# ACT reads a finished product sum one instruction earlier, ahead of the last score tile's exponential, in thirteen stretches of a fused attention and token-mixer kernel

## The chip, the cores and the metric

One Trainium2 chip, one core of it. The metric is the device time of the kernel in microseconds (us), the median of several runs, so lower is better. Names of the engines: PE is the matrix engine, PEld its weight-load port, DVE the vector engine, ACT the scalar (activation) engine, POOL the GpSimd engine, SP the engine that issues the DMAs.

## The reference

Two branches read the same tokens `x` (2048 tokens, 640 channels) and a gate per token mixes them. Branch A is attention with 32 query heads of width 20 that share one key and one value head. Branch B is a token mixer: a layer norm, then an MLP across the token axis.

```python
# A: q is (32 heads, 2048, 20), k and v are (2048, 20), all from x
scores = jnp.einsum("bhqd,bkd->bhqk", q, k) * (Dh ** -0.5)
p = _softmax(scores, axis=-1)
a = (jnp.einsum("bhqk,bkd->bhqd", p, v)) ... @ wo
# B: h is layernorm(x); u is (640, 1728), y is (640, 2048)
u = _gelu(jnp.einsum("bsd,sf->bdf", h, w1) + b1)
y = jnp.einsum("bdf,fs->bds", u, w2) + b2
g = _sigmoid((x * gate_w).sum(-1, keepdims=True))
out = g * a + (1 - g) * y.transpose
```

Everything is float32. The kernel splits the operands of most products into a high and a low part, so each product becomes three matmuls that add into one PSUM tile.

## The kernel before, in words

The order of every engine's instructions is written out by hand (a manual schedule over all five engines): an engine executes them in the order in which the Python code emits them, and waits where an operand or a buffer isn't ready.

After a first part that makes q, k, v and the layer norm, the kernel runs a list `ph` of 326 **stretches**. `main(k, vs)` emits stretch k. It has two lanes on PE, one for each half of the rows of the array, and `merged` interleaves them by modelled times:

- One lane holds twelve 512-column matmuls: six that recompute scores for the row maxima (`ms_next`, line 479, each followed by a DVE reduction, line 482) and six that compute score tiles (`s_next`, which calls `qk`, line 657, each followed by the exponential on ACT, line 660, which reads the score tile from PSUM and writes a tile `p`).
- The other lane holds about sixteen matmuls of branch B (the "fill"), here line 750: pieces of y = W2 u for one block of 128 tokens. They add into the PSUM tile `g`.

A stretch ends with the products p times v of one or two finished score units (`pv_mm`, line 684): one unit when k is even, two when k is odd.

Three points matter for the change.

1. The product sum `g` has one PSUM bank only (`ps_g`, one buffer). For the first thirteen token blocks (`st < FIVE`) each of the two channel halves (d = 0 and d = 1) takes five stretches (`five(d)`). At the end of the fifth, `done(d)` (line 758) makes ACT read `g` with scale and bias into the tile `yo`. The next stretch starts a new sum in the same bank, so its first fill matmul waits for that read. For d = 0 the fifth stretch has an even k, for d = 1 an odd one.
2. The score tiles and the tiles of the row maxima go round six PSUM banks in turn (`next_bank`: three named `ms`, three named `s`). A matmul into a bank waits until the reader of the tile six calls before has finished.
3. `done` stands in the order after the fill, and the last score step of the stretch stands ahead of the last fill matmul. So ACT gets: exponential, exponential of the last score tile, then the read of `g`.

Of the kernel before, what the change touches and what calls it, by code (L numbers as in the profile page):

```python
# [11 lines left out]
AF = mybir.ActivationFunctionType  # L12
# [23 lines left out]
SCALE = DH ** -0.5  # L36
# [3 lines left out]
def mix_kernel(ctx: ExitStack, tc: tile.TileContext, A_x, A_wq, A_wk, A_wv, A_wo,  # L40
               B_x, B_w1, B_b1, B_w2, B_b2, gate_w, out):
    nc = tc.nc
# [3 lines left out]
    def f32(ap):  # L46
        return ap.bitcast(F32)
# [107 lines left out]
    def new_q(n):  # L155
        if n < NU:
            qtiles[n] = load_q(n, "qst")
# [13 lines left out]
    with tc.tile_pool(name="pa", bufs=1) as pa, \  # L171
# [129 lines left out]
        def q_parts(m, ts):  # L301
            cols = slice(m * P, (m + 1) * P)
            return [[(wq_hi[:, c, cols], ts[c][0]) for c in range(DC)],
                    [(wq_hi[:, c, cols], ts[c][1]) for c in range(DC)],
                    [(wq_lo[:, c, cols], ts[c][0]) for c in (0, 3, 1, 4, 2)]]
# [88 lines left out]
        for sb in range(NQB):  # L394
# [11 lines left out]
            for m in range(DC):  # L406
# [3 lines left out]
                p = q_parts(m, ts)  # L410
# [48 lines left out]
    def next_bank():  # L459
        if not ring:  # L460
            return ps_m.tile([P, NB], F32, name="ms")
        ring[0] ^= 1
        return ps_m.tile([P, NB], F32, name="ms") if ring[0] else ps_s.tile([P, NB], F32, name="s")
# [25 lines left out]
    def ms_done():  # L489
        n = len(row_max)  # L490
        if n < NU and min(issued) >= 32 * (n + 1):
            mm = mmpool.tile([P, 16], F32, name="mm")
            nc.vector.tensor_reduce(mm, mtiles.pop(n), axis=AX.X, op=ALU.max)
            mn = mmpool.tile([P, 2, 16], F32R, name="mn")
            nc.gpsimd.tensor_scalar(mm, mm, -1.0, None, op0=ALU.mult)
            nc.gpsimd.tensor_copy(mn[:, 0, :], mm)
            nc.gpsimd.tensor_sub(mn[:, 1, :], mm, f32(mn[:, 0, :]))
            row_max[n] = mn
# [66 lines left out]
    with tc.tile_pool(name="psb", bufs=2, space=PSUM, side="right") as psb:  # L565
# [8 lines left out]
        for fc in range(PRO):  # L574
            pu = [psb.tile([P, NB], F32, name=f"pu{r}") for r in range(2)]
            for hf in range(4):
# [4 lines left out]
                for c in range(HS):  # L581
# [6 lines left out]
                    done = [max(0, min(x, last) - skip) * LEAD // (last - skip) for x in (at, at + 1)]  # L588
# [45 lines left out]
    SYNC = mybir.DependencyInfo(mybir.DependencyClass.Sync, mybir.DependencyReason.DATA)  # L634
    sc = [0, 0]
    turn_p = [0]

    def next_p():
        turn_p[0] += spare[0]
        i = turn_p[0] % 14  # L640
        return extra_p[i - 1] if 0 < i < 4 else pp_pool.tile([P, NB], F32, name="p")

    def s_next(b):
        j = sc[b]
        if j >= 2 * len(units):
            return None
        sc[b] += 1
        return lambda: qk(j // 2, j % 2, b)

    def qk(u, pr, b):  # L650
        n, kb = units[u]
        assert n in back_in
        if kb == 4 and pr == 0 and b == 0:
            new_q(n + 1)
        q = qtiles[n]
        s = ps_s.tile([P, NB], F32, name="s") if spare[0] else next_bank()
        nc.tensor.matmul(s, kst[64 * b:64 * b + 62, kb * P:(kb + 1) * P], q[64 * b:64 * b + 62, pr, :],  # L657
                         start=True, stop=True)
        p = next_p()
        nc.scalar.activation(p, s, AF.Exp, scale=SCALE)  # L660
        ptiles[u, 2 * pr + b] = p

    def other_tile(half, ins):
        if half is not None and last["half"] not in (half, None):
            tc.add_manual_dep(ins.ins, last["sig"].ins.name, SYNC, reason="row tiles that share a bank")
        last["half"], last["ins"] = half, ins
# [11 lines left out]
    def pv_mm(u):  # L678
        n, kb = units[u]
        if kb == 0:  # L680
            otile[0] = ps_o.tile([P, NB], F32, name="o")
        o = otile[0]
        for hh in range(4):
            nc.tensor.matmul(o[32 * hh:32 * hh + 32, :], v_sb[:, kb, :], ptiles.pop((u, hh)),  # L684
                             start=(kb == 0), stop=(kb == NS - 1), skip_group_check=True)
        if kb == NS - 1:
            qb, g = divmod(n, NQ)
            ot = ev.tile([P, NB // 32, 32], F32, name="ot")
            rl = ev.tile([P, NB // 32], F32, name="rl")
            on = ev.tile([P, NB], F32, name="on")  # L690
            oh = ev.tile([P, NB], F32R, name="oh")
            ol = ev.tile([P, NB], F32R, name="ol")
            direct = spare[0]
            src = o
            if not direct:
                src = on
                nc.scalar.activation(src, o, AF.Copy)

            def turn():
                nc.vector.transpose(ot.rearrange("p c e -> p (c e)"), src)  # L700

            def scale():
                if not direct:
                    turn()
                nc.vector.reciprocal(rl, ot[:, :, DH])  # L705
                (nc.vector if spare[0] else nc.gpsimd).tensor_mul(ot, ot, rl[:, :, None].to_broadcast([P, NB // 32, 32]))  # L706

            if direct:
                turn()

            def back():
                nc.vector.transpose(on, ot.rearrange("p c e -> p (c e)"))

            def high():
                osplit[:] = [oh, ol]
                if n < NU - 1:
                    nc.gpsimd.tensor_copy(oh, on)
                else:
                    nc.scalar.activation(oh, on, AF.Copy)

            def low():
                (nc.vector if n == NU - 1 else nc.gpsimd).tensor_sub(ol, on, f32(oh))
                for j, t in enumerate((oh, ol) if n < NU - 1 else ()):
                    for hh in range(4):
                        r = (4 * g + hh) * DH
                        nc.sync.dma_start(out=o_scr[j, r:r + DH, qb * NB:(qb + 1) * NB],
                                          in_=f32(t[32 * hh:32 * hh + DH, :]))

            if direct:
                later.append((False, None))  # L730
            later.extend(((True, scale), (True, back), (False, high), (False, low)))
# [222 lines left out]
    for i, (steps, rest, done) in enumerate(seq):  # L954
        item, j = divmod(i + 1, 3)
        rest.insert(0, lambda c=4 * (PRO + item) + (48 * j // 3) // 12: w1_upto(c + 4))
    def stretches(seq):
        return [(rows[1 - b], rest if b else [], done if b else []) for rows, rest, done in seq for b in range(2)]

    ph = stretches(seq)  # L960
# [29 lines left out]
    def merged(lx, lf):  # L990
        lanes, at, out = (list(lx), list(lf)), [0.0, 0.0], []
        while lanes[0] or lanes[1]:
            k = 0 if lanes[0] and (not lanes[1] or at[0] <= at[1]) else 1
            us, f = lanes[k].pop(0)
            if f:
                out.append(f)
            at[k] += us
        return out
# [18 lines left out]
    def main(k, vs):  # L1017
        b = k % 2
        fs, rest, done = ph[k]
        fill = [(F_US, f) for f in fs] + [(0.0, f) for f in [signal] + done]  # L1020
        if not vs:
            lx = [(3 * X_US, ms_next(b)), (3 * X_US, ms_next(b)), (X_US, s_next(b)), (X_US, ms_next(b))]
            lx += [(X_US, s_next(b)) for _ in range(3)]
            lf = fill + [(X_US, s_next(1 - b))]
        else:
            sx, sf = (MANY if len(fs) > 15 else FEW)[len(vs) == 1]
            lx = [(X_US, (s_next if c == "s" else ms_next)(b)) for c in sx]
            lf = []
            for c in sf:
                lf += fill if c == "F" else [(X_US, (s_next if c == "s" else ms_next)(1 - b))]  # L1030
        order = merged(lx, lf)
        known, kept = set(row_max), set(sent)
        wide = len(vs) == 2
        parted = wide and units[vs[0]][1] == NS - 1
        for i, f in enumerate(order):
            if wide and i == (len(order) + 1) // 2:
                settle()
                if parted:
                    pv_mm(vs[0])
            f()  # L1040
        ms_done()
        spare[0] = len(row_max) == NU
        settle(wide and not parted)
        if vs:
            n, kb = units[vs[0]][0] + 1, units[vs[0]][1]
            if n in kept and n not in back_in:
                fetch_max(n)
                back_in.add(n)
        for f in rest:
            f()  # L1050
        if vs and kb > 4 and n in known and n not in sent and n < NU:
            store_max(n)
            sent.add(n)
        for v in vs[parted:]:
            pv_mm(v)
# [16 lines left out]
    for n in BLOCKS:  # L1072
# [3 lines left out]
        i = 0  # L1076
        while any(sc[b] < ends[b] for b in range(2)):
            b = int(sc[1] < sc[0])
# [3 lines left out]
        fs = [tail_take(b, len(tail[b]) if n == left else  # L1082
                        max(0, round(((own[b] + len(tail[b]) * F_US) * n / left - len(lanes[b]) * X_US) / F_US)))
              for b in range(2)]
        at = [0.0, 0.0]
        while any(lanes) or any(fs):
            b = 0 if at[0] <= at[1] and (lanes[0] or fs[0]) or not (lanes[1] or fs[1]) else 1
# [76 lines left out]
```

## Time and profile before

| | |
|---|---|
| Time, median of 3 runs | 1671.76 us (1671.31 to 1671.92) |
| The profiled execution's own time | 1671.47 us |
| Its span, first to last instruction | 1669.7 us |
| Granted TensorE clock | 1.000 |
| Busy: PE / PEld / DVE / ACT / POOL | 99% / 66% / 86% / 71% / 36% |
| The stretches of the d = 0 and d = 1 sums above | about 689 to 1262 us of the span |

A row of the timeline reads: start in us, length in us, engine, line, operation, output<-inputs, shapes, count; in brackets stands how long the engine was idle before it, and what ended that. Matmuls are pipelined and overlap, so the sum of their lengths says little; their starts tell the rhythm.

### The profile page before, as it was taken

The numbers are of one execution on the slowest core, as the hardware profiler recorded it, in microseconds if no ns is written. First come the engines' busy times: TensorE is split into PE (matmuls) and PEld (weight loads), VectorE is DVE, ScalarE is ACT, GpSimd is POOL, SyncE is SP. The second block draws the span as 40 slices with busy tenths as digits, with TensorE's granted clock in tenths as the row PEclk, the third lists the DMA queues.
The fourth block names the chain that finished last, engine by engine and source line by source line (L and its number), as shares of the span: only waits on it lengthen the run. The fifth ranks groups of instructions, "written<-read, shape, count | busy, mean of one in ns | idle before, by whom it ended". The sixth has DMA issues, their size and how long they took to land.

```text
span 1669.7 us, 38827 instructions
## 1 busy us (share of the span) xinstructions
PE 1661.0 (99%) x14865; PEld 1105.5 (66%) x14865; DVE 1435.7 (86%) x2732; ACT 1188.0 (71%) x2346; POOL 606.3 (36%) x759
## 2 busy tenths in 40 slices
PE   9999999999999999999999999999999999999998
PEld 7899666666666666666666666666666566666665
DVE  6689899999989999988888988988888998988933
ACT  4434777777777777777777777777777777777775
POOL 6578555455455554422232332122122220111210
PEclk9999999999999999999999999999999999999999
DMA  7665222222132232222222222212222121333611
GB/s 211 205 176 137 79 71 69 78 58 78 53 84 73 71 82 74 58 60 62 66 75 74 55 62 66 61 52 71 63 66 60 55 65 41 96 111 113 189 51 39
DMA packets 178305, 138.20 MB, mean 83 GB/s; under 512 B 33306, under 2 KB 144055, under 8 KB 178119
## 3 DMA queue, kind: packets, MB, share of 16 engines
q1 hardware_dynamic: 177830, 135.39, 28.9%
q8 instruction: 117, 1.92, 0.5%
q14 instruction: 70, 0.57, 0.1%
q10 hardware_dynamic: 288, 0.33, 0.1%
HBM read 102.36 MB, written 31.65 MB: 80 GB/s over the span
## 4 chain that ended last, share of the span: by engine, by line
PE 95%; issue 2%; DVE 1%; SPq 1%; ACT 0%; DMA 0%; POOL 0%; POOLq 0%; DVEq 0%; ACTq 0%
PE o L684 28%; PE ms L479 18%; PE s L657 13%; PE g L750 10%; PE g L929 7%; PE ms L657 5%; PE pp L298 4%; PE s L479 3%; PE pu L586 3%; PE g L875 2%; DVE mp L482 1%; PE ms L831 0%; ACT p L660 0%; PE pt L290 0%; SPq L195 0%
## 5 line engine op out<-in xcount | busy, mean ns | idle before, releaser
L482 DVE TENSOR_REDUCE mp<-ms 128x1 f32<-128x512 f32 x1514 | 967.2, 685 | 130.2 <-PE ms L479 102.7
L660 ACT ACTIVATE p<-s 128x512 f32<-128x512 f32 x1512 | 820.6, 606 | 299.4 <-PE s L657 280.2
L479 PE MATMUL ms<-kst,qmx 60*128 60x512 f32 x1514 | 646.5, 433 | 1.7 <-DVE mp L482 1.7
L657 PE MATMUL s<-qst,kst 62*128 62x512 f32 x1512 | 601.6, 403 | 0.0
L684 PE MATMUL o<-p,v_sb 128*32 128x512 f32 x4096 | 511.3, 601 | 0.0
L479 PEld LDWEIGHTS ms<-kst,qmx 60*128 60x128 f32 x1514 | 279.0, 184 | 244.9 <-ACT p L660 114.7
L482 DVE TENSOR_REDUCE mp<-s 128x1 f32<-128x512 f32 x534 | 355.6, 683 | 12.0 <-PE s L479 11.8
L660 ACT ACTIVATE p<-ms 128x512 f32<-128x512 f32 x536 | 305.1, 599 | 56.8 <-PE ms L657 50.2
L657 PEld LDWEIGHTS s<-qst,kst 62*128 62x128 f32 x1512 | 278.5, 186 | 55.2 <-DVE flag L670 31.0
L929 PE MATMUL g<-slot,wh 64*128 64x320 f32 x1280 | 297.5, 311 | 0.0
L129 POOL TENSOR_TENSOR wl<-wr,wh 128x512 fp32r<-128x512 f32 x176 | 228.6, 1300 | 43.8 <-PE g L750 17.3
L479 PE MATMUL s<-kst,qmx 60*128 60x512 f32 x534 | 230.8, 441 | 0.4 <-DVE yo L525 0.4
L684 PEld LDWEIGHTS o<-p,v_sb 128*32 128x32 f32 x4096 | 97.5, 108 | 185.3 <-issue 177.2
L657 PE MATMUL ms<-qst,kst 62*128 62x512 f32 x536 | 216.8, 405 | 0.0
L929 PEld LDWEIGHTS g<-slot,wh 64*128 64x128 f32 x1280 | 211.6, 184 | 2.0 <-issue 1.7
L750 PE MATMUL g<-slot,wh 64*128 64x320 f32 x864 | 202.1, 313 | 0.1
L750 PE MATMUL g<-u,wh 64*128 64x320 f32 x864 | 201.7, 312 | 0.0
L929 PE MATMUL g<-slot,wl 64*128 64x320 f32 x640 | 199.6, 312 | 0.0
L706 POOL TENSOR_TENSOR ot<-ot,rl 128x512 f32<-128x512 f32 x30 | 31.6, 1052 | 346.6 <-DVE rl L705 346.6
L128 POOL CAST wh<-wr 128x512 fp32r<-128x512 f32 x144 | 88.3, 613 | 188.0 <-PE g L750 81.5
L750 PEld LDWEIGHTS g<-slot,wh 64*128 64x128 f32 x864 | 143.5, 184 | 4.9 <-ACT yo L758 4.0
L750 PEld LDWEIGHTS g<-u,wh 64*128 64x128 f32 x864 | 143.5, 184 | 1.1 <-issue 1.1
(202 smaller groups left out, 2092.8 us busy)
## 6 DMA issues: line engine op xcount, KB each, us to landing
wr<-in_B_w_dram SPq DMA_DIRECT2D x152, 256.0 KB
qmx<-q_scr SPq DMA_DIRECT2D x192, 80.0 KB
qst<-q_scr SPq DMA_DIRECT2D x192, 80.0 KB
slot<-o_scr SPq DMA_DIRECT2D x20, 320.0 KB
y_scr<-yo SPq DMA_DIRECT2D x16, 320.0 KB
o_scr<-oh SPq DMA_DIRECT2D x124, 40.0 KB
o_scr<-ol SPq DMA_DIRECT2D x124, 40.0 KB
q_scr<-qh SPq DMA_DIRECT2D x19, 256.0 KB
```

The costliest lines, as they stand in the source:

```text
L128: nc.gpsimd.tensor_copy(wh, wr)
L129: nc.gpsimd.tensor_sub(wl, wr, f32(wh))
L298: nc.tensor.matmul(pp, w, t, start=first and n == 0, stop=not more and n == len(steps) - 1)
L479: nc.tensor.matmul(ms, qmax[n][64 * b:64 * b + 60, pr, qt * P:(qt + 1) * P], kst[64 * b:64 * b + 60, kq * NB:(kq + 1) * NB], start=True, s ...
L482: nc.vector.tensor_reduce(mtiles[n][:, c, kq:kq + 1], ms, axis=AX.X, op=ALU.max)
L586: nc.tensor.matmul(pu[r][:, :HD2], w[rows, c, :], h[rows, st, :], start=(st == 0 and k == 0), stop=(st == NS - 1 and k == 2))
L657: nc.tensor.matmul(s, kst[64 * b:64 * b + 62, kb * P:(kb + 1) * P], q[64 * b:64 * b + 62, pr, :], start=True, stop=True)
L660: nc.scalar.activation(p, s, AF.Exp, scale=SCALE)
L684: nc.tensor.matmul(o[32 * hh:32 * hh + 32, :], v_sb[:, kb, :], ptiles.pop((u, hh)), start=(kb == 0), stop=(kb == NS - 1), skip_group_check ...
L750: other_tile(half, nc.tensor.matmul(hold["p"][:, :HD2], w[r, fc % HS, :], u[d][r, fc, :], start=(hold["n"] == 1), stop=(hold["n"] == 6 * F ...
L875: other_tile(half, nc.tensor.matmul(hold["p"][:, :HD2], o[r, c, :], w[r, c, d * HD2:(d + 1) * HD2], start=(hold["n"] == 1), stop=(hold["n" ...
L929: other_tile(half, nc.tensor.matmul(hold["p"][:, :HD2], w[r, st % HS, :], h[d][r, st, :], start=(hold["n"] == 1), stop=(hold["n"] == 6 * NS)))
```

## The change

In `main`, for a stretch that ends a sum, has an even k, p v units to do and over fifteen fill matmuls, the last score step ahead of `done[0]` is marked. Its matmul is emitted where it was; its exponential is kept back until `done[0]` has emitted ACT's read of `g`, and is emitted right behind it. These are the d = 0 sums of the thirteen first token blocks.

```diff
@@ s_next
-        return lambda: qk(j // 2, j % 2, b)
+
+        def step():
+            qk(j // 2, j % 2, b)
+
+        step.score = True
+        return step
@@ qk
         p = next_p()
-        nc.scalar.activation(p, s, AF.Exp, scale=SCALE)
         ptiles[u, 2 * pr + b] = p
+
+        def exp():
+            nc.scalar.activation(p, s, AF.Exp, scale=SCALE)
+
+        if delayed:
+            delayed.append(exp)
+        else:
+            exp()
@@ main
         order = merged(lx, lf)
+        scores = [f for f in order if getattr(f, "score", False)]
...
+        hold = None
+        if done and vs and not k + 1 >= len(ph) and k % 2 == 0 and len(fs) > 15:
+            hold = [i for i, f in enumerate(order[:order.index(done[0])]) if f in scores][-1]
         for i, f in enumerate(order):
...
+            if i == hold:
+                delayed.append(None)
             f()
+            if hold is not None and f is done[0]:
+                delayed.pop(1)()
+                delayed.clear()
```

In the built program the order on PE, DVE, POOL and SP is the same as before. On ACT thirteen pairs are exchanged: "exponential, read of g" becomes "read of g, exponential". On PE thirteen score matmuls (line 657), the second of the stretch after each exchanged pair, get a wait for ACT that they did not have.

More of the change, by code (lines that the diff above doesn't have):

```diff
@@ L636, in mix_kernel @@
     turn_p = [0]
+    delayed = []
     def next_p():
```

## The prediction, made before the changed kernel was run

> **What bounds the kernel now.** I read the page's busy shares first, then its chain, then the waits of the line that the change moves, then the timeline at one of the thirteen places and at an undisturbed stretch beside it.
>
> ```profile
> PE 1661.0 (99%) x14865; PEld 1105.5 (66%) x14865; DVE 1435.7 (86%) x2732; ACT 1188.0 (71%) x2346; POOL 606.3 (36%) x759
> PE 95%; issue 2%; DVE 1%; SPq 1%; ACT 0%; DMA 0%; POOL 0%; POOLq 0%; DVEq 0%; ACTq 0%
> ```
>
> PE carries the kernel from end to end: 95% of the chain that ended last is PE. ACT is busy for 71% and hardly on the chain. So a reordering on ACT can only pay where PE waits for ACT. At first sight PE has no such time, it is 99% busy; but this busy time is a union of overlapping matmuls whose ends are modelled, and a late start inside it need not show. The starts of the weight loads (PEld) show the rhythm better. The instructions of line 758 (ACT's read of g), over the stretch that holds all thirteen places:
>
> ```profile
> L758 ACT ACTIVATE yo<-g,b2g,og_half x25: 642/643/645, 710.6 to 1239.7; 128x320 f32<-128x320 f32 x25
>   PEld ms L479: 9.2, 11
>   PEld g L750: 4.0, 13
> ```
>
> The last two rows are who waited for it. Thirteen weight loads of g did, 4.0 us in all: the thirteen sums that the change treats. The 9.2 us of line 479 are something else: every stretch begins with a 0.84 us pause of the load port while PE works off the p times v products, whatever is named as its end, as the rows of undisturbed stretches below show. Here is the first of the thirteen places:
>
> ```profile
> 709.10 0.39 PE L657 MATMUL s<-qst,kst 62*128 62x512 f32 x1
> 709.20 0.30 PE L750 MATMUL g<-u,wl 64*128 64x320 f32 x1
> ...
> 709.62 1.09 ACT L660 ACTIVATE p<-s 128x512 f32<-128x512 f32 x2
> ...
> 710.58 0.64 ACT L758 ACTIVATE yo<-g,b2g,og_half 128x320 f32<-128x320 f32 x1
> 710.80 0.18 PEld L479 LDWEIGHTS ms<-kst,qmx 60*128 60x128 f32 x1 [0.84 <-ACT p L660]
> ...
> 711.27 0.18 PEld L750 LDWEIGHTS g<-slot,wh 64*128 64x128 f32 x1 [0.29 <-ACT yo L758]
> ...
> 711.87 0.60 ACT L660 ACTIVATE p<-s 128x512 f32<-128x512 f32 x1 [0.65 <-PE s L657]
> ```
>
> The last matmul of the old sum ends at 709.50. ACT is then behind by two exponentials (709.62 and, in the same row of two, the last score tile's), reads g from 710.58 to 711.22, and the new sum's first weight load goes at 711.27, 0.05 after. The new stretch had begun at 710.80. In an undisturbed stretch with the same number of matmuls the load of g goes at once:
>
> ```profile
> 719.95 0.18 PEld L479 LDWEIGHTS ms<-kst,qmx 60*128 60x128 f32 x1 [0.84 <-ACT p L660]
> 719.95 0.18 PEld L750 LDWEIGHTS g<-slot,wh 64*128 64x128 f32 x1
> 720.05 0.19 PEld L657 LDWEIGHTS s<-qst,kst 62*128 62x128 f32 x1
> ...
> 720.52 0.19 PEld L657 LDWEIGHTS s<-qst,kst 62*128 62x128 f32 x1
> ```
>
> So at each place the load of g comes 711.27 - 710.80 = 0.47 late, and the score matmul behind it in PE's queue with it.
>
> **What the wait costs.** Neither 4.0 us (idle of a port) nor 13 x 0.47 = 6.1 us (lateness) is the loss, because the two lanes overlap again afterwards. The loss is the length of the stretch, from one first load to the next. For the first of the thirteen, an undisturbed one, the last full one, the worst one and the short one (split by the end of a query block), with a short undisturbed one last, I read these starts; those of 710.80 and 719.95 stand above:
>
> ```profile
> 715.90 0.18 PEld L479 LDWEIGHTS ms<-kst,qmx 60*128 60x128 f32 x1 [0.84 <-issue]
> 724.71 0.18 PEld L479 LDWEIGHTS ms<-kst,qmx 60*128 60x128 f32 x1 [0.84 <-issue]
> 1239.89 0.18 PEld L479 LDWEIGHTS ms<-kst,qmx 60*128 60x128 f32 x1 [0.84 <-ACT p L660]
> 1240.38 0.18 PEld L750 LDWEIGHTS g<-slot,wh 64*128 64x128 f32 x1 [0.31 <-ACT yo L758]
> 1245.01 0.18 PEld L479 LDWEIGHTS ms<-kst,qmx 60*128 60x128 f32 x1 [0.84 <-issue]
> 931.55 0.18 PEld L479 LDWEIGHTS ms<-kst,qmx 60*128 60x128 f32 x1 [0.84 <-ACT p L660]
> 932.10 0.18 PEld L750 LDWEIGHTS g<-slot,wh 64*128 64x128 f32 x1 [0.36 <-ACT yo L758]
> 936.74 0.18 PEld L479 LDWEIGHTS ms<-kst,qmx 60*128 60x128 f32 x1 [0.84 <-issue]
> 1195.59 0.18 PEld L479 LDWEIGHTS ms<-kst,qmx 60*128 60x128 f32 x1 [0.84 <-ACT p L660]
> 1196.08 0.18 PEld L750 LDWEIGHTS g<-slot,wh 64*128 64x128 f32 x1 [0.31 <-ACT yo L758]
> 1198.59 0.18 PEld L750 LDWEIGHTS g<-slot,wh 64*128 64x128 f32 x1 [0.84 <-issue]
> 772.55 0.18 PEld L479 LDWEIGHTS ms<-kst,qmx 60*128 60x128 f32 x1 [0.84 <-ACT p L660]
> 775.14 0.18 PEld L750 LDWEIGHTS g<-slot,wl 64*128 64x128 f32 x1 [0.84 <-issue]
> ```
>
> Undisturbed: 724.71 - 719.95 = 4.76. First: 715.90 - 710.80 = 5.10, so 0.34 lost. Last full one: 5.12, 0.36 lost. Worst: 5.19, 0.43 lost at a lateness of 932.10 - 931.55 = 0.55. Short: 3.00 against 2.59, 0.41 lost. The loads of g come 0.47, 0.49, 0.55 and 0.49 late; in all four the loss is the lateness less 0.08 to 0.13 us, which the lanes absorb. Eleven ordinary places at 0.34 to 0.36 are 3.7 to 4.0; with the worst and the short one 4.6 to 4.8 us. I take 4.7.
>
> **What the change moves.** At each place two ACT instructions change places; the number of instructions on every engine stays. Part by part:
>
> 1. *The read of g starts earlier.* It takes the kept-back exponential's slot. That row of two exponentials is 1.09 long and one alone is 0.60, so the second starts 1.09 - 0.60 = 0.49 after the first; the read follows by about as much again (710.58 less 709.62 is 0.96, two slots). So it moves from 710.58 to 710.10, ends at 710.74, and the load of g is free at 710.79: the stretch begins at 710.80. It just fits. At the worst place 932.10 - 0.48 = 931.62 against 931.55: still 0.07 late, within the 0.08 that lanes absorbed. Residue: 0 to 0.1 us over all thirteen; I take 0.
> 2. *Is g ready then?* The moved read waits for the last matmul of the sum, 709.20 + 0.30 = 709.50; ACT comes to it at 710.10, 0.6 later. So ACT doesn't stand at it, and nothing queues behind it.
> 3. *The last score tile's exponential starts later*, behind the read. What follows a read of g directly on ACT is seen once:
>
> ```profile
> 1151.43 0.64 ACT L758 ACTIVATE yo<-g,b2g,og_half 128x320 f32<-128x320 f32 x1
> 1151.93 0.63 ACT L697 ACTIVATE on<-o 128x512 f32<-128x512 f32 x1
> ```
>
> The next instruction starts 0.50 behind it. So the exponential starts at 710.10 + 0.50 = 710.60 in place of 710.10 and ends at 711.20 in place of 710.70. No later ACT work is pushed: ACT then idles (0.65 us before 711.87).
> 4. *Who waits for it: the new wait.* Its score bank goes, six tiles on, to the second score matmul of the next stretch (line 657), whose weight load in the undisturbed stretch comes 720.52 - 719.95 = 0.57 after the start, so here at 710.80 + 0.57 = 711.37. With the 0.05 of passing on, the bank is free at 711.25: 0.12 in hand, at the worst place, whose stretch begins nearly 0.07 sooner after the read, about 0.05. Behind that load stand all later matmuls of PE, so if it is late, the stretch is late. What an exponential directly behind a read of g costs, no row shows. Lower bound 0.50 (the row above). Upper bound 0.64, no overlap at all: the exponential then ends at 711.34, the bank is free at 711.39, 0.02 late at an ordinary place and 0.09 at the worst, at most 0.3 us over thirteen even if nothing is absorbed. I take 0.50, since that row is the same read with the next instruction waiting, hence a cost of zero; it can't be a gain, because nobody takes the tile sooner. The Trainium skill (ScalarE: Activation LUTs, "What ACT_TABLE_LOAD costs") lets back-to-back activations overlap by about 93 ns. By that the follower would start 0.55 behind the read, an estimate; this case's row has 0.50, an overlap of 0.14, and either leaves the bank free in time.
> 5. *The tile `p` itself* is multiplied at the end of the next stretch, nearly 5 us later; 0.5 us don't matter there.
> 6. *Nothing crosses a queue of SP, POOL or DVE*: they keep their order. The new wait rides on one weight load each.
>
> The saving is worth its full size only if nothing else sets PE's pace after it. Undisturbed stretches with the same matmuls run at 4.76 in the same region with the same DVE, POOL and DMA work, so these do not.
>
> **Sum.** 1671.47 us of the profiled execution less 4.7 is 1666.8. That execution lies 0.3 below the median of 1671.76, so against the median 1667.1. A measurement tells about 0.2% from no change here, 3.3 us.
>
> **The rivals.**
>
> *The stall changes its place.* The score bank, not g, becomes what the stretch waits for. Against it speak the 0.12 in hand and the bounds in step 4; for it, that the margin is a tenth of a microsecond, and that it is worked out from one pair of rows. It decides from an exponential that ends over 0.2 us later than worked out. If that exponential started a full slot later still (0.48 more), its load would be 0.48 - 0.12 = 0.36 late, less 0.1 absorbed 0.26, times 13 = 3.4 us given back: 1670.5, "same".
>
> *The wait for g is not what lengthens the stretch.* The stretch after a finished sum might be longer for another reason, such as the other weights it starts on. Then nothing changes: 1671.8. Against it: the long stretch follows exactly the thirteen reads that were waited for, the start at 719.95 is on the same kind of weights, and the loss grows with lateness (0.34 at 0.47, 0.43 at 0.55). The Trainium skill (Perfetto Trace Analysis, "Identifying the Most-Contended Engine") advises to work first on the engine with the highest occupancy, and excepts the matrix engine, whose matmul busy share it calls no good measure of how near it is to its limit. Taken without the exception it would make a shift on ACT, at 71%, worth nothing. The load that comes 0.47 late inside a PE that is 99% busy speaks for the exception.
>
> *Slower: ACT stands at the head of its queue.* If the sum were finished only after ACT came to the read, ACT would wait with the exponential behind it. It begins to bite from a sum that ends over 0.6 us later against ACT than now, and it is worse than before from 1.1 us, where the read is back at its old place. With ACT held for 1.0 us at each place the load of g would come 710.79 + 1.0 = 711.79, 0.99 late; less 0.12 absorbed 0.87, times 13 = 11.3; less the 4.7 that was lost already, 6.6 slower: 1678.4. The trace has 0.6 us in hand against it.
>
> *The change doesn't do what it says* can be left aside: the built order shows thirteen exchanged pairs and no other.
>
> **Chances.** Forecast 0.78 (1667.1, own range 1666.3 to 1668.3 by residue and bounds); stall in the other place, in part or whole, 0.12; no effect 0.05; slower 0.05. A part of the second case still saves over 3.3 us: faster 0.79, same 0.16, slower 0.05. The range goes up to 1669.8 to take in half of the second case, and down to 1666.0 for the scatter of the runs (0.3 either way) beyond 4.8 saved and what the split stretch might add.
>
> **What would show it.** In the changed kernel's profile: the row "PEld g L750" among those who waited for the read of g gone or under 0.5 us (step 1); the thirteen stretches at 4.76 instead of 5.10 to 5.19; the read starting one exponential behind the exponential before it, without idle time (step 2); its follower 0.50 behind it (step 3); no new row "PEld s L657 <- ACT p L660" of a microsecond or more (step 4). Wrong would be: stretches at 4.76 and the same total, so that a later wait took the gain; or a wait of line 657 in the place of line 750's.

## The result, and the profile after

| | before | after |
|---|---|---|
| Median of 7 runs | 1671.59 us (1671.08 to 1671.92) | 1666.11 us (1665.75 to 1667.19) |
| Span of the profiled execution | 1669.7 us | 1664.3 us |
| Ratio of the times, 95% interval | | 0.9968 (0.9959 to 0.9977) |

The kernel is 5.5 us faster. Forecast were 1667.1 us, 4.7 us faster, in a range of 1666.0 to 1669.8: the time lies in that range, 0.1 above its lower end, but 0.2 below the forecast's own, narrower range of 1666.3 to 1668.3. So the size of the gain was forecast a little too small; why, the last experiments and the account below them say.

The busy shares and the chain of the page after look as before; the gain can't be read from them. PE is busy for 99% again, of a shorter span:

```profile
PE 1655.7 (99%) x14865; PEld 1103.8 (66%) x14865; DVE 1434.6 (86%) x2732; ACT 1187.1 (71%) x2346; POOL 605.3 (36%) x759
PE 96%; issue 2%; DVE 1%; ACT 0%; POOL 0%; POOLq 0%; DVEq 0%; ACTq 0%
```

The read of g (now line 771) and who waited for it, over the same part of the kernel:

```profile
L771 ACT ACTIVATE yo<-g,b2g,og_half x25: 632/632/645, 709.9 to 1234.6; 128x320 f32<-128x320 f32 x25
  PEld ms L479: 20.1, 24
```

The row of thirteen waiting weight loads of g, 4.0 us, is gone. The 20.1 us of line 479 are not a new wait: that is the 0.84 us pause that begins every stretch, 24 of them, of which 13 used to be put down to the exponential and now to the read, because the last ACT instruction that finished before them is another one.

The first of the thirteen places in the timeline after:

```profile
709.00 0.30 PE L763 MATMUL g<-u,wl 64*128 64x320 f32 x1
...
709.42 0.60 ACT L669 ACTIVATE p<-s 128x512 f32<-128x512 f32 x1
709.89 0.63 ACT L771 ACTIVATE yo<-g,b2g,og_half 128x320 f32<-128x320 f32 x1
710.39 0.62 ACT L669 ACTIVATE p<-s 128x512 f32<-128x512 f32 x1
710.58 0.18 PEld L479 LDWEIGHTS ms<-kst,qmx 60*128 60x128 f32 x1 [0.84 <-ACT yo L771]
710.58 0.18 PEld L763 LDWEIGHTS g<-slot,wh 64*128 64x128 f32 x1
...
711.15 0.19 PEld L663 LDWEIGHTS s<-qst,kst 62*128 62x128 f32 x1
...
711.34 0.60 ACT L669 ACTIVATE p<-s 128x512 f32<-128x512 f32 x1 [0.33 <-PE s L663]
```

The read starts one slot (0.47 us) behind the exponential ahead of it and ends at 710.52. The stretch begins at 710.58, and the load of g goes with it. The kept-back exponential starts 0.50 behind the read, ends at 711.01, and the load of the score matmul that needs its bank, 711.15, does not wait.

The lengths of the thirteen stretches, from first load to first load, at the same places as before (the first, the worst, the short one and the last):

```profile
715.33 0.18 PEld L479 LDWEIGHTS ms<-kst,qmx 60*128 60x128 f32 x1 [0.84 <-issue]
929.47 0.18 PEld L479 LDWEIGHTS ms<-kst,qmx 60*128 60x128 f32 x1 [0.84 <-ACT yo L771]
934.23 0.18 PEld L479 LDWEIGHTS ms<-kst,qmx 60*128 60x128 f32 x1 [0.84 <-issue]
1191.41 0.18 PEld L479 LDWEIGHTS ms<-kst,qmx 60*128 60x128 f32 x1 [0.84 <-ACT yo L771]
1194.00 0.18 PEld L763 LDWEIGHTS g<-slot,wh 64*128 64x128 f32 x1 [0.84 <-issue]
1235.32 0.18 PEld L479 LDWEIGHTS ms<-kst,qmx 60*128 60x128 f32 x1 [0.84 <-ACT yo L771]
1240.09 0.18 PEld L479 LDWEIGHTS ms<-kst,qmx 60*128 60x128 f32 x1 [0.84 <-issue]
```

They are 4.75, 4.76, 2.59 and 4.77 us, against 5.10, 5.19, 3.00 and 5.12 before. Of the nine not shown, eight lie between 4.75 and 4.77. The third of the thirteen is 4.81: there a load of line 479, late in the stretch, waits 0.15 us for DVE, as it did not before, so a later wait took 0.05 of the gain back at this one place. I added up all thirteen in both traces, start to start: 64.50 before, 59.76 after, **4.75 us** less. The two spans differ by 5.33. Of the other 0.6 us, 0.28 lie ahead of the first stretch that I measured (177 us, in a part that the change does not touch), and 0.30 net in the other stretches, most of it in three long ones, which the experiments take up.

### The profile page after: what moved, and what is told of

Its sections match the earlier page's. It is cut to its first block, busy times and chain, and to the rows that moved or that the text cites. A ratio compares the mean times of both kernels' runs of the same rounds, so it can differ in the third digit from the quotient of the medians.

```text
span 1664.3 us, 38815 instructions
## 1 busy us (share of the span) xinstructions
PE 1655.7 (99%) x14865; PEld 1103.8 (66%) x14865; DVE 1434.6 (86%) x2732; ACT 1187.1 (71%) x2346; POOL 605.3 (36%) x759
## 4 chain that ended last, share of the span: by engine, by line
PE 96%; issue 2%; DVE 1%; ACT 0%; POOL 0%; POOLq 0%; DVEq 0%; ACTq 0%
PE o L697 29%; PE ms L479 18%; PE s L663 13%; PE g L763 10%; PE g L942 7%; PE ms L663 5%; PE pp L298 4%; PE s L479 3%; PE pu L586 3%; PE g L888 2%; DVE mp L482 1%; PE ms L844 0%; PE pt L290 0%; PE pp L362 0%; ACT p L669 0%
```

## The experiments

Each edit is against the changed kernel, unless it says otherwise. The kernel before was timed on the same chip beside each of them; its medians are named where they matter.

### The read at its old time, in the new order

The exponential ahead of the read is computed twice, into the same tile.

```diff
         else:
             exp()
+            last_exp[0] = exp
...
             if i == hold:
+                last_exp[0]()
                 delayed.append(None)
             f()
```

> The order of the changed kernel (read of g ahead of the last score tile's exponential), but the exponential ahead of it is computed twice, into the same tile, at the thirteen places; the result is the same. So the read starts where it started before the change, one exponential later. Theory (the lateness of the read is all that the change removed): the load of g is 0.47 us late again, the thirteen stretches are 5.10 to 5.15 long, and the time is that of the kernel before, 1671.6 (1671.0 to 1672.2). Rival (the order, the new waits or the place of the instructions made the gain, not the time of the read): 1666 to 1667.

Measured: 1672.91 us (1672.51 to 1675.42), the kernel before beside it 1671.34; ratio 1.0011 (1.0002 to 1.0020). The gain is gone, so the rival (order or placing) is out. It is even 1.6 us slower than before, above the expected range; the thirteen stretches alone are 2.0 us longer than before. The trace shows why:

```profile
710.11 1.23 ACT L670 ACTIVATE p<-s 128x512 f32<-128x512 f32 x2
711.24 0.61 ACT L773 ACTIVATE yo<-g,b2g,og_half 128x320 f32<-128x320 f32 x1
711.26 0.18 PEld L479 LDWEIGHTS ms<-kst,qmx 60*128 60x128 f32 x1 [0.84 <-ACT p L670]
711.90 0.18 PEld L765 LDWEIGHTS g<-slot,wh 64*128 64x128 f32 x1 [0.46 <-ACT yo L773]
```

Two exponentials into one tile take 1.23 instead of 1.09 us: the second starts 0.64 behind the first, when that has ended (it is 0.60 long), and not 0.48. So the read is later than it ever was before: it starts 0.02 ahead of the stretch, where it had started 0.22 ahead; the load of g comes 711.90 - 711.26 = 0.64 late, and the full stretches are 5.26 to 5.28 long, with one of 5.35 (the eleventh, where ACT has another instruction behind the pair). Lateness 0.64, loss 0.52: the same 0.12 us absorbed as in the prediction's rows. This is a third point on its line (0.34 at 0.47, 0.43 at 0.55, 0.52 at 0.64). The kept-back exponential is late here as well and holds the second score load until 712.39; but the third score load comes 0.83 behind the load of g, as before (0.82), so this second wait adds nothing.

### Six places of thirteen

```diff
-        if done and vs and not k + 1 >= len(ph) and k % 2 == 0 and len(fs) > 15:
+        if done and vs and not k + 1 >= len(ph) and k % 2 == 0 and len(fs) > 15 and k < len(todo) * 6 + 60:
```

> The exchange at the first six of the thirteen places only. Theory (each place pays for itself): the first six stretches are 4.76, the other seven 5.10 to 5.2; the first six lost 2.1 us in the trace of before, so 1669.4 (1669.0 to 1669.9). Rival (the part of the measured gain beyond the thirteen stretches, 0.6 us, belongs to the change and comes with the first exchanges): 1668.8 or less. Rival (a later wait takes part of it back, only the sum counts): 1670 or more.

Measured: 1668.91 us (1668.53 to 1670.33), 2.4 us below the 1671.34 beside it; ratio 0.9986 (0.9977 to 0.9995). The first six stretches are 4.76 to 4.81, the last seven 5.10 to 5.12 with the short one at 3.00; the waits name seven loads of g:

```profile
PEld g L763 <- ACT yo L771: 2.1, 7, 0.3
```

The thirteen add up to 62.29 us, 2.2 less than before. Each place pays for itself, and nothing later takes it back. The absolute time is a tenth below the expected range, and the kernel before was itself 0.25 lower here. Against the kernel beside it the gain is 2.4 us, where the theory said 2.2 and the first rival 2.8 or more: too close to say whose the 0.6 us are. The traces below do.

### The kept-back exponential made later

A copy of yo onto itself stands between the read and the exponential.

```diff
                                  bias=b2g[:, st:st + 1], scale=og_half[:, st:st + 1])
+            again[0] = lambda: nc.scalar.activation(t[:, d * HD2:(d + 1) * HD2], t[:, d * HD2:(d + 1) * HD2], AF.Copy)
...
             if hold is not None and f is done[0]:
+                again[0]()
                 delayed.pop(1)()
```

> The changed kernel with a copy of yo onto itself (128x320) on ACT between the read of g and the kept-back exponential at the thirteen places. The read of g stays early, the exponential ends about 0.5 us later than in the changed kernel. Theory (the score bank of that exponential is the next thing to be late, with about 0.1 us in hand and 0.1 absorbed): its load is about 0.4 us late, 0.3 us per stretch, 13 x 0.3 = 3.9 us: 1670.0 (1668.7 to 1671.0), with weight loads of line 657 waiting for ACT. Rival (that bank has far more in hand, only the bank of g counts): 1666.1 to 1666.6.

Measured: 1669.34 us (1668.87 to 1670.23), 3.2 above the changed kernel; ratio to before 0.9988 (0.9979 to 0.9997). In the first place:

```profile
709.76 0.63 ACT L772 ACTIVATE yo<-g,b2g,og_half 128x320 f32<-128x320 f32 x1
710.42 0.47 ACT L774 ACTIVATE yo<-yo 128x320 f32<-128x320 f32 x1
710.43 0.18 PEld L479 LDWEIGHTS ms<-kst,qmx 60*128 60x128 f32 x1 [0.84 <-ACT yo L772]
710.80 1.07 ACT L670 ACTIVATE p<-s 128x512 f32<-128x512 f32 x2
711.43 0.18 PEld L664 LDWEIGHTS s<-qst,kst 62*128 62x128 f32 x1 [0.25 <-ACT p L670]
```

and over the part with the thirteen places:

```profile
PEld s L664 <- ACT p L670: 3.2, 13, 0.3
```

So the prediction's first rival exists: the score bank is the next thing to be late, at all thirteen places. The load comes 711.43 - 710.43 = 1.00 after the start of the stretch instead of 0.57, so 0.43 late, but the ordinary stretches are only 4.93 to 4.95 long, 0.18 lost (the eleventh is 5.22, the short one 2.89). A late score load costs less than a late load of g: 0.25 us are absorbed, not the 0.1 that I had carried over. The thirteen stretches are 2.7 us longer than in the changed kernel; two pauses of ACT, of the kind described below, add 0.4.

### Two exponentials kept back

```diff
-            hold = [i for i, f in enumerate(order[:order.index(done[0])]) if f in scores][-1]
+            hold = [i for i, f in enumerate(order[:order.index(done[0])]) if f in scores][-2]
...
-                delayed.pop(1)()
+                for f in delayed[1:]:
+                    f()
```

> Two exponentials kept back behind the read of g in place of one, at the thirteen places. The read starts another 0.48 us earlier, 0.1 us after the sum is finished. Theory (no load of g is late any more after the change, so an earlier read brings nothing, and the second exponential ends where it ended): as the changed kernel, 1666.1 (1665.6 to 1666.8), the thirteen stretches at 4.76. Rival (some lateness of g is left in the changed kernel): up to 0.5 us faster, 1665.6 or less. Rival (ACT stands at the unfinished sum): slower by over 1 us.

Measured: 1666.12 us (1665.71 to 1666.68); ratio to before 0.9968 (0.9957 to 0.9980). The thirteen stretches add up to 59.74, against 59.76 in the changed kernel. Half a microsecond more of earliness is worth nothing: the change had already removed all of the lateness.

### Three exponentials kept back

As above with `[-3]`.

> Three exponentials kept back behind the read of g at the thirteen places. ACT comes to the read at about 0.4 us before the sum is finished and stands there with the three exponentials behind it. Theory (the head-of-queue case of the prediction, small): the read starts about 0.1 us after the sum's end, the three exponentials end 0.4 us later than in the changed kernel, the score banks of the last two are 0.3 us late, 0.2 to 0.3 us per stretch: 2.8 to 4.3 us slower than the changed kernel, 1669.0 to 1670.4, with ACT idle ahead of the read. Rival (score banks have slack enough): 1666.1 to 1666.6.

Measured: 1668.67 us (1668.12 to 1669.65), 2.5 above the changed kernel; ratio to before 0.9983 (0.9974 to 0.9992). That is 0.3 below the expected range, but the mechanism is the expected one:

```profile
709.16 1.11 ACT L669 ACTIVATE p<-s 128x512 f32<-128x512 f32 x2
710.55 0.62 ACT L771 ACTIVATE yo<-g,b2g,og_half 128x320 f32<-128x320 f32 x1 [0.28 <-PE g L763]
711.07 0.59 ACT L669 ACTIVATE p<-ms 128x512 f32<-128x512 f32 x1
711.55 1.09 ACT L669 ACTIVATE p<-s 128x512 f32<-128x512 f32 x2
711.79 0.18 PEld L479 LDWEIGHTS ms<-kst,qmx 60*128 60x128 f32 x1 [0.84 <-DVE flag L683]
...
712.20 0.18 PEld L663 LDWEIGHTS s<-qst,kst 62*128 62x128 f32 x1
```

```profile
ACT yo L771 <- PE g L763: 3.6, 12, 0.4
```

ACT stands in front of the unfinished sum with three exponentials behind it, by name at twelve of the places. The full stretches are 4.87 to 4.94 long, with one of 5.13, so 0.12 to 0.18 is lost at an ordinary place where I had expected 0.2 to 0.3. The first score load comes 712.20 - 711.79 = 0.40 after the start of the stretch instead of 0.10, 0.30 late: here 0.18 us were absorbed. The thirteen stretches are 2.0 us longer than in the changed kernel; two pauses of ACT, described below, add 0.4.

### The exchange wherever a sum ends

```diff
-        if done and vs and not k + 1 >= len(ph) and k % 2 == 0 and len(fs) > 15:
+        if done and vs and not k + 1 >= len(ph):
```

> The exchange at every stretch that ends a product sum (71 places: also the d = 1 sums, the first MLP product and the output projection), not at the thirteen alone. Theory (an exchange pays only where the read was waited for): beside the thirteen, the trace of before shows one stretch, at 777 us, with 0.26 us lost to a waited read, and one of 0.07 us at 1339; so 0.0 to 0.4 us faster than the changed kernel, 1665.7 to 1666.3. Rival (every earlier read is worth something): 71/13 of 4.7, over 15 us faster. Rival (elsewhere the kept-back exponential is what the next stretch needs): slower than 1666.8.

Measured: 1665.67 us (1665.12 to 1666.37), ratio to before 0.9964 (0.9952 to 0.9977): the lowest median of all, 0.4 us below that of the changed kernel, which was timed apart from it. Repeated beside it on one chip:

> The changed kernel again, beside the next one: 1666.1 (1665.7 to 1666.6).

> The exchange at all 71 stretches that end a sum, again, beside the changed kernel on the same chip. If its lead of 0.4 us is the one waited read at 777 us and the like, it is 0.2 to 0.5 us below the changed kernel again; if it was scatter, 0 to 0.2 either way.

There the changed kernel took 1667.38 us (1665.78 to 1667.77; ratio to before 0.9962, 0.9949 to 0.9974), this one 1666.04 (1665.92 to 1667.68; 0.9960, 0.9947 to 0.9972), the kernel before 1673.09. The medians are 1.3 us apart, more than any of the expectations, but on this chip the runs of one kernel scatter by 2 to 4 us, and the times alone do not decide. The traces do: three stretches differ by over 0.03 us in all traces of the two kernels. One is the stretch at 777 us that the expectation named. Before, its load of g came 0.40 late, 0.07 behind the end of the read (777.28 + 0.64):

```profile
777.28 0.64 ACT L758 ACTIVATE yo<-g,b2g,og_half 128x320 f32<-128x320 f32 x1
777.59 0.18 PEld L479 LDWEIGHTS ms<-kst,qmx 60*128 60x128 f32 x1 [0.84 <-ACT p L660]
777.99 0.18 PEld L750 LDWEIGHTS g<-u,wh 64*128 64x128 f32 x1 [0.21 <-issue]
781.75 0.18 PEld L479 LDWEIGHTS ms<-kst,qmx 60*128 60x128 f32 x1 [0.84 <-ACT p L660]
```

With the exchange there too:

```profile
776.25 0.18 PEld L479 LDWEIGHTS ms<-kst,qmx 60*128 60x128 f32 x1 [0.84 <-ACT yo L771]
776.25 0.18 PEld L763 LDWEIGHTS g<-u,wh 64*128 64x128 f32 x1
780.15 0.18 PEld L479 LDWEIGHTS ms<-kst,qmx 60*128 60x128 f32 x1 [0.84 <-ACT p L669]
```

4.16 became 3.90. The other two, at 220 and 637 us in the first MLP product, went from 4.03 and 4.04 to 3.90; in the one at 220 the load of g had been 0.27 late (220.79 against 220.52), a loss of 0.13, again on the line. Together 0.5 us; the other 55 of the 71 exchanges changed no length by over 0.03 us. An exchange pays only where the read was waited for.

### Second traces of both kernels, and the missing 0.6 us

> The kernel before once more, for a second trace. The spans of the two traces differ by 5.3 us, of which 4.75 lie in the thirteen stretches; 0.28 lie in the first 177 us and 0.65 in single stretches at 927, 1400 and 1525 us. Theory (these are differences of one execution): in this trace those three stretches are at their neighbours' lengths, others may be long, and the thirteen are again 0.34 to 0.43 too long (worst place: 0.36, since its 0.43 came from the hiccup at 927). Rival: the three stretches are long again, so the change shortens them too.

> The changed kernel once more, for a second trace. The thirteen stretches are 4.75 to 4.81 long again. If the 0.6 us beyond them come from single executions, this trace has single long stretches somewhere or a longer start; if they belong to the change, the three stretches at 927, 1400 and 1525 us are at their neighbours' lengths here too.

Measured, one execution of each: 1671.67 and 1666.14 us. Here my theory fell. The three long stretches of before (0.21, 0.25 and 0.28 us, at 927, 1400 and 1525 us) are there again, at the same instructions, and the changed kernel has none of them, both times. The stretch behind the one at 1525 is 0.09 shorter in before, so the three cost 0.65 us net. In each of them ACT starts an exponential 0.19 to 0.21 us late, and the profile puts the wait down to a matmul of g, which an exponential does not read; at 927 us this is the same instruction in the first and in the second trace of before:

```profile
928.20 1.09 ACT L660 ACTIVATE p<-s 128x512 f32<-128x512 f32 x2 [1.69 <-PE s L657]
929.48 0.60 ACT L660 ACTIVATE p<-s 128x512 f32<-128x512 f32 x1 [0.19 <-PE g L750]
```

```profile
928.33 1.09 ACT L660 ACTIVATE p<-s 128x512 f32<-128x512 f32 x2 [1.70 <-PE s L657]
929.61 0.60 ACT L660 ACTIVATE p<-s 128x512 f32<-128x512 f32 x1 [0.19 <-PE g L750]
```

and the same place in the changed kernel, without a pause:

```profile
926.34 1.59 ACT L669 ACTIVATE p<-s 128x512 f32<-128x512 f32 x3 [1.69 <-PE s L663]
```

The pause at 929.48 is also what made the "worst" of the thirteen places the worst: the read behind it came that much later. Shortly after it, at 930.1, the trace has one packet of 8 KB on an instruction queue (q14). To see whether the place depends on how many ACT instructions come before, I put forty one-element copies on ACT far ahead, into the kernel before and into the changed one:

```diff
+    dum = const.tile([1, 1], F32, name="dum")
...
+        if 10 <= k < 50:
+            nc.scalar.activation(dum, dum, AF.Copy)
         ms_done()
```

> The kernel before with forty one-element copies more on ACT, one per stretch, between 200 and 400 us, where ACT is idle for part of each stretch; nothing else is changed. In both traces of the kernel before, ACT starts one exponential 0.19 us late in three stretches (927, 1400 and 1525 us), the same three instructions both times, about 0.6 us ahead of an 8 KB packet on an instruction queue; they cost 0.8 us together. Theory (ACT pauses where its instruction stream passes from one block to the next, so the place depends on the count of ACT instructions ahead of it): these three pauses go, others may come elsewhere; the time is 1670.7 to 1672.2, and the thirteen stretches stay at 5.1 to 5.2 but for those with a pause. Rival (the pauses belong to these places): they stay at the same three exponentials.

> The changed kernel with the same forty one-element copies on ACT. It has no such pause that shows in a stretch's length. Theory (their absence is luck of the count): long stretches of 0.2 to 0.3 us may come, none to four; the time is 1665.9 to 1667.1, the thirteen stretches stay at 4.76. Rival (the change itself removes them): none comes, 1666.1.

Measured, on the scattering chip: 1672.35 us beside 1673.09 for the kernel before (ratio 0.9996, 0.9987 to 1.0005), and 1668.68 (ratio to before 0.9976, 0.9966 to 0.9986) beside 1667.38 for the changed kernel. Both are above the expected times, as are the medians of the two kernels beside them. The traces speak more clearly. In the kernel before the long stretches at 927, 1400 and 1525 are gone, and others have come (0.15 us more in the fourth of the thirteen, 0.21 at 1190). In the changed kernel, which had none, there are three: at 779, 984 and 1260 us, 0.22 to 0.26 each. Its thirteen stretches stay at 59.74 us.

So the pauses go by the count of ACT's instructions, not by the place in the work. The traces show the count itself. Between 700 and 1600 us, all fourteen traces together have seventeen exponentials ahead of which ACT is idle for 0.14 to 0.22 us and for which the profile names a matmul of g. The number of ACT records ahead of such an exponential in the trace (EVENT_SEMAPHORE, the waiting instruction, counted too) is 63 more than a multiple of 128 at all seventeen: 1599, 2495 and 2751 at 927, 1400 and 1525 us in both traces of before. At all seventeen the record just ahead is an EVENT_SEMAPHORE; most other places of this grid show no pause. The long stretch at 779 us in the changed kernel with the copies fits as well: its late exponential is record 1343 (63 more than ten times 128), with ACT idle for 1.01 us ahead of it, against 0.73 at the same place in the changed kernel. The seventeen are in seven different kernels; there is none in the changed kernel, in the one that keeps two exponentials back and in the one with 71 exchanges. Fourteen of them have an 8 KB packet of q14 0.57 to 0.93 us behind their start; the two at 1525 us have none so near, and one in the kernel before with the copies has it 1.15 behind. That the pauses stand on a grid of 128 ACT instructions is shown; that ACT passes there from one block of instructions to the next fits it, but is argued, not shown.

## Why the prediction was right

*What bounds the kernel, and what a waited read costs:* right. The sum over thirteen stretches was forecast at 4.7 and measured at 4.75 us. Of the 0.43 lost at the worst place, 0.07 go with a pause of ACT ahead of it, which the forecast took for part of the wait. Reading lengths of stretches rather than waits was the decisive choice: the wait row (4.0) and the lateness (6.1) both miss it.

*Step 1, it just fits:* right. Forecast was a load free within 0.01 us of the start of the stretch; it goes at 710.58 with it. The residue of 0.07 at the worst place did not come, since that place is no different from the others without the pause ahead of it. That the pause is not there in the changed kernel is luck of the count.

*Step 2, g is ready:* right; three exponentials, not one or two, must be kept back until ACT stands in front of the sum.

*Steps 3 and 4, the follower and its bank:* right in size. The exponential starts 0.50 behind the read, as taken. By the Trainium skill (ScalarE: Activation LUTs, "What ACT_TABLE_LOAD costs"), which lets back-to-back activations overlap by about 93 ns, an estimate with the 0.63 us of the row is 0.54; the trace has 0.50, an overlap of 0.13. In hand are 711.15 less 711.06 (the end of the exponential and 0.05 of passing on), 0.09 us, where 0.12 was worked out. The price of missing it was set too high: I took 0.1 us to be absorbed, and the kernel with the copy of yo shows 0.25.

*Nothing else sets PE's pace after it:* right at twelve places; at the third a wait for DVE took 0.05 us back.

*The rival "no effect"* fell with the first run, and with it the reading that a shift on ACT, busy for 71%, can give nothing while PE is busy for 99%: PE had 4.75 us to give. On this the trace agrees with the exception that the Trainium skill makes for the matrix engine (Perfetto Trace Analysis, "Identifying the Most-Contended Engine").

*What the sum lacked:* 1.0 us between 1667.1 and 1666.11. About 0.2 of it is the median of before, which came out at 1671.59 and not at 1671.76, and another 0.2 that the medians lie further apart (5.48) than the profiled spans (5.33) and the thirteen gave 0.05 more. The other 0.6 is in the trace, outside the thirteen stretches. I took these stretches as unchanged, because I compared the thirteen with undisturbed neighbours and never listed which other stretches were long. In before three were, by 0.65 us net, each behind a pause of ACT; the changed kernel has none. In the first pair of traces the other stretches give 0.36 of it back in differences of thousandths, in the second pair 0.17. This part of the gain is not the exchange's doing: forty idle copies bring three such pauses into the changed kernel as well. The rest, 0.28 us, lies ahead of 177 us, where neither kernel differs. The first two traces of each kernel agree on it within 0.02 us, but a third trace of the changed kernel has that start 1.3 us later, and over all traces it lies anywhere from 176.5 to 180.1. So I put no weight on it, and its cause stays open. The mechanism was right, then; that the total still fell into the range, with pauses in it that no term foresaw, is owed to the margin for scatter.

## What to carry to other kernels

Where two lanes share an in-order engine, the cost of a late operand is neither the wait that the profile names nor the lateness, but the longer stretch: measure from start to start against an undisturbed neighbour. On an engine that is not the bottleneck, put first the instruction whose result the bottleneck needs first, and stop as soon as nothing waits for it; the next step further (three exponentials here) makes it wait itself. When differences of 0.05% matter, list every long stretch before taking a gain for the edit's own: here pauses that move with the instruction count were worth an eighth of this one.

## What the runs showed of the hardware

Two activations in a row of 512 columns start 0.48 us apart, but 0.64 apart when the second writes the tile that the first writes (1.23 for the two instead of 1.09). After the read, an independent follower starts 0.50 behind, one that reads the result 0.66 behind (709.76 to 710.42). ACT pauses of 0.14 to 0.22 us stand at places 128 of its instructions apart (seventeen of seventeen, all behind an EVENT_SEMAPHORE), and the stretches with them are 0.15 to 0.28 us longer. A late weight load that feeds the fill lane costs its lateness less 0.12 to 0.14 us at six of the seven places read here (0.08 at the seventh, the short stretch), one that feeds the score lane its lateness less 0.18 to 0.25 (two places).
